# First batch's chunk loop: score matmuls two chunks ahead, weight conversions moved behind the loop, unread matmuls in every chunk

## The chip, the cores and the metric
The kernel runs on one core of one Trainium2 chip. The metric is the device time of one execution in microseconds. Five engines work side by side, each through its own list of instructions in order: PE (matmuls), DVE (vector), ACT (scalar functions), POOL (GpSimd) and SP, which here only starts transfers. An engine waits at an instruction until its inputs are there and its output buffer is free; what stands behind it on the same engine waits too.

## What is computed
The reference has three steps, for 4 batches of 768 positions with 8 heads of 48 channels (384 channels together). All is fp32.

```
# 1. scan over the positions t, for each head; a is complex, scaled to at most 0.999
S_re, S_im = ar*S_re - ai*S_im + outer(k_t, v_t),  ar*S_im + ai*S_re
y_t = q_t @ S_re
# 2. Fourier mixing over positions and channels, then a channel MLP
u = y + real(fft(fft(y, positions), channels))
z = u + relu(layernorm(u) @ w_ch1) @ w_ch2
# 3. a token MLP, then a channel MLP
z = z + (relu(z.T @ w_tok1) @ w_tok2).T
out = z + relu(z @ w_ch1') @ w_ch2'
```

## The kernel before, in words
**The scan.** The decay is the same for all positions of a short step, so the kernel first works out running products of `a` on DVE, ACT and POOL (for the next batch while the dense layers of this one run: the instructions around L558 to L615, of which L571 on POOL and L577 on DVE come early). Then the 768 positions are taken as 8 chunks of 96. A chunk `c` has four parts:
- `ch_load(c)`: SP starts the loads of V and of the scaled keys Kn. V has two buffers, so V(c+2) is loaded when the output of chunk c has been computed.
- `ch_sc(c)`: eight score matmuls q·k on PE (L753, two groups of four; a fp32 matmul shows as two entries in the trace, so one chunk is x16), and two masks on DVE (L760).
- `ch_u(c)`: V·K on PE (L768, L769) and then the state: DVE adds the old state (L779, `Aa`) and scales it (L785 `Xx`, L786 `yc`), POOL scales the other half (L787), DVE adds up the new state `T` (L789). Each chunk's state needs the one before: this is the chain of the loop.
- `ch_y(c)`: scores·V (L802) and q·T (L808) on PE, and ACT writes the chunk's output into `xT` (L810). After it stands `warm(n, ident)` where the table `WC` has a number n: n matmuls of 128x128 into a PSUM buffer that nobody reads (L309).

**Weight conversion.** The MLP weights come as fp64 bit patterns and are turned into two fp32r parts, high and low, in scratch memory. One conversion handles 128x384 weights: a 384 KB load by SP (L185), ACT L191 and L192, DVE L194, POOL L196, DVE L199, ACT L205, POOL L206, and a store by SP. Each needs the one before. Twenty of them (8 `early`, 12 `back`) are spread over the first batch; `tick` moves each running conversion on by one part and starts n new ones, `loads` starts only their loads, and `feed(n)` runs whatever of the twenty is left, in full. `CF[0]` are started ahead of the loop and `CF[c+1]` in chunk c. The other 36 are converted during the first dense layer.

**Stage 2, first batch.** `xT` is folded by sums and differences (`xf` L982, `xd` L988, `fd` L999; half on DVE, half on POOL for the first two), transformed by matmuls on PE (L1022, then L1033), copied out by ACT (L1069) and combined on POOL (L1070, L1071: three pairs). DVE joins that with the transposed x into u (L1085), takes mean and variance (L1092, L1093), refines the inverse root (L1104 to L1108) and normalizes (L1114), in three rounds. The normalized tiles are transposed on PE (L906), split by ACT (`th`, L909) and DVE (`tl`, L910), and the first MLP starts (L926, then ACT L930 and DVE L932; second layer L942).

**What sets the order.** The code is not run in the written order: a list scheduler with its own timeline orders each engine's instructions, and buffers come from pools by tag. `rests` and `after` are hints of order alone: in the loop, L194 and L199 come behind the chunk's T, and L196 behind its L787.

Of the kernel before, what the change touches and what calls it, by code (L numbers as in the profile page):

```python
# [26 lines left out]
SL4 = [(N4 * i, N4) for i in range(12)] + [(48, 1)]  # L27
ACL = 0.999
W0, WS = 2, 8
CF = (2, 2, 2, 2, 2, 0, 8, 0)  # L30
AN = (5, 6, 6, None)
WC = (0, 0, 0, 0, 0, 0, 10, 12)
WZ, CL = 0, 1
XL = (0,), (0, 1, 2, 3, 4, 5)
AH = 4
# [18 lines left out]
def attn_fft_mixer_kernel(ctx: ExitStack, tc: tile.TileContext, aL, xL, vL, wL, qN, kN, vN, arN, aiN,  # L54
# [37 lines left out]
    def alloc(tag, shape, dt=F32, name=None):  # L92
        n = 1
        for x in shape[1:]:
            n *= x
        t = pool.tile([128, SIZE[tag]], dt, tag=tag, bufs=BUFS[tag], name=name or tag)
        return shaped(t[0:shape[0], 0:n], shape)
# [3 lines left out]
    def palloc(tag, shape):  # L101
        n = 1
        for s in shape[1:]:
            n *= s
        t = psum.tile([128, 512], F32, tag=tag, bufs=PSB[tag], name=tag)
        v = t[0:shape[0], 0:n]
        if len(shape) == 3:
            v = v.rearrange("p (a b) -> p a b", b=shape[2])
        return v
# [107 lines left out]
    def begin():  # L217
        p, j = convs.pop(0)
        return convert(p, j, ws.place if (p, j) in early else None)
# [10 lines left out]
    def tick(n, loads=False):  # L230

        keep, stream[0] = stream[0], BACK
        active[:] = [g for g in active if next(g, "end") != "end"]
        for _ in range(n):
            g = begin()
            next(g)
            if not loads:
                next(g)
            active.append(g)
        stream[0] = keep  # L240
# [64 lines left out]
    def warm(n, x):  # L305

        ps = palloc("l", [128, 512])
        for _ in range(n):
            te.matmul(out=ps[:, 0:x.shape[1]], lhsT=ident[0:x.shape[0], :], rhs=x)  # L309
# [391 lines left out]
    def stage1(b):  # L701
# [9 lines left out]
        def st_g2():  # L711
            ps = palloc("s", [112, 4, 64])
            gt = alloc("e", [112, 3, 2, 64], name="gt")
            f47 = t[0]["ends"][:, 0].rearrange("p c f -> p (c f)")
            f48 = t[0]["ends"][:, 1].rearrange("p c f -> p (c f)")
            for j, (src, o, sel) in enumerate(((f47, 0, 64), (f47, 48, 64), (f48, 0, 0), (f48, 48, 0))):
                for r0 in (0, 64):
                    te.matmul(out=ps[r0:r0 + 48, j, :], lhsT=src[:, o:o + 48], rhs=ident[:, sel:sel + 64])

            def v(ap, r0):  # L720
                return ap[r0:r0 + 48].rearrange("p k (h c) -> p k h c", c=8)
            for r0 in (0, 64):
                fs, t1, t2, g = (v(x, r0) for x in (gt[:, 0], gt[:, 1], gt[:, 2], gm[b % 2]))
                se.copy(out=gt[r0:r0 + 48, 0], in_=ps[r0:r0 + 48, 0:2, :])
                bq = v(ps[:, 2:4, :], r0)
                ve.tensor_tensor(out=t1[:, :, :, 0:7], in0=fs[:, :, :, 0:7], in1=bq[:, :, :, 1:8], op=ALU.mult)
                for kk in range(2):
                    ve.tensor_tensor(out=t2[:, kk, :, 0:7], in0=fs[:, kk, :, 0:7], in1=bq[:, 1 - kk, :, 1:8], op=ALU.mult)
                ve.tensor_tensor(out=g[:, 0, :, 0:7], in0=t1[:, 0, :, 0:7], in1=t1[:, 1, :, 0:7], op=ALU.add)
                s0, s1 = (0, 1) if r0 == 0 else (1, 0)  # L730
                ve.tensor_tensor(out=g[:, 1, :, 0:7], in0=t2[:, s0, :, 0:7], in1=t2[:, s1, :, 0:7], op=ALU.subtract)
            fl = palloc("s", [128, 1])
            te.matmul(out=fl, lhsT=allones, rhs=good)
            ve.tensor_scalar(out=gate[:, b:b + 1], in0=fl, scalar1=127.5, scalar2=None, op0=ALU.is_ge)

        st = {}
        PU = "l" if b == 0 else "s"

        def ch_load(c):
            v = alloc("P", [96, 384], name="V")  # L740
            sp.dma_start(out=v, in_=vL[b, c])
            kt = alloc("A", [96, 8, 128], name="Kn")
            for hf in range(2):
                sp.dma_start(out=kt[48 * hf:48 * hf + 48],
                             in_=knd[hf].rearrange("(h c) s f -> c s h f", c=8)[c])
            st[c] = dict(v=v, kt=kt)

        def ch_sc(c, half):
            ps = palloc("s", [96, 4, 96])
            Q, K = qk[0][:, 1], qk[0][:, 0]  # L750
            for j in range(4):
                hc = (half * 4 + j) * 8 + c
                te.matmul(out=ps[:, j, :], lhsT=K[:, hc, :], rhs=Q[:, hc, :])  # L753
            sc = alloc("e", [96, 4, 96], name="sc")
            mb = mask.unsqueeze(1).to_broadcast([96, 4, 96])
            if half and OFF[2] & (1 << b):
                se.copy(out=sc, in_=ps)
                ge.tensor_tensor(out=sc, in0=sc, in1=mb, op=ALU.mult)
            else:
                ve.tensor_tensor(out=sc, in0=ps, in1=mb, op=ALU.mult)  # L760
            st[c][f"sc{half}"] = sc

        def ch_u(c):
            d = st[c]
            ps = palloc(PU, [112, 8, 48])
            for h in range(8):
                vv = d["v"][:, h * 48:h * 48 + 48]
                te.matmul(out=ps[0:64, h, :], lhsT=d["kt"][:, h, 0:64], rhs=vv)  # L768
                te.matmul(out=ps[64:112, h, :], lhsT=d["kt"][:, h, 64:112], rhs=vv)  # L769
            g = gm[b % 2].rearrange("p k (h c) -> p k h c", c=8)[:, :, :, c:c + 1]  # L770

            def gb(k, lo, hi):
                return g[lo:hi, k].to_broadcast([hi - lo, 8, 48])

            def v8(ap):
                return ap.rearrange("p (h e) -> p h e", e=48)
            if c:
                a = alloc("e", [112, 384], name="Aa")
                ve.tensor_tensor(out=v8(a), in0=v8(st["T"]), in1=ps, op=ALU.add)  # L779
                a = v8(a)  # L780
            else:
                a = ps
            y = yc[c % 2]
            x = alloc("e", [112, 384], name="Xx")
            ve.tensor_tensor(out=v8(x), in0=a, in1=gb(0, 0, 112), op=ALU.mult)  # L785
            (ge if c and b else ve).tensor_tensor(out=v8(y)[0:48], in0=a[64:112], in1=gb(1, 64, 112), op=ALU.mult)  # L786
            st["yop"] = (ge if c else ve).tensor_tensor(out=v8(y)[64:112], in0=a[0:48], in1=gb(1, 0, 48), op=ALU.mult)  # L787
            T = alloc("e", [112, 384], name="T")
            st["op"] = ve.tensor_tensor(out=T, in0=x, in1=y, op=ALU.add)  # L789
            st["Tn"] = T  # L790
            if b == 0:
                tops.append(st["op"])

        def ch_y(c):
            d = st[c]
            Q = qk[0][:, 1]
            ps = palloc(PU, [112, 4, 96])
            for p in range(4):
                for k in range(2):
                    h = 2 * p + k  # L800
                    m = 48 if k else 64
                    te.matmul(out=ps[64 * k:64 * k + m, p, :], lhsT=d["v"][:, h * 48:h * 48 + m],  # L802
                              rhs=d[f"sc{h // 4}"][:, h % 4, :], start=True, stop=(c == 0))
                if c:
                    for k in range(2):
                        h = 2 * p + k
                        m = 48 if k else 64
                        te.matmul(out=ps[64 * k:64 * k + m, p, :], lhsT=st["T"][:, h * 48:h * 48 + m],  # L808
                                  rhs=Q[:, h * 8 + c, :], start=False, stop=True)
            marked(se.activation(out=xT[:, :, c * 96:c * 96 + 96], in_=ps, func=ACTF.Copy, scale=gate[0:112, b:b + 1]))  # L810

        if b == 0:
            tick(CF[0])
        st_g2()
        ch_load(0)
        ch_load(1)
        ch_sc(0, 0)
        ch_sc(0, 1)
        for c in range(8):
            if c < 7:  # L820
                ch_u(c)
                ch_sc(c + 1, 0)
                ch_sc(c + 1, 1)
            ch_y(c)
            if b == 0 and WC[c]:
                warm(WC[c], ident)
            st["T"] = st.get("Tn")
            if c < 6:
                ch_load(c + 2)
            if b == 0 and c < 7:  # L830
                rests[0], rests[1] = tops[c], st["yop"]
                tick(CF[c + 1], c == 5)

# [120 lines left out]
    def stage2(b):  # L954
# [53 lines left out]
        if b == 0:  # L1008
            marked(x)
            rests[0], rests[1] = x, None  # L1010
            for _ in range(5):
                tick(0)
            rests[0] = None
# [38 lines left out]
        st = alloc("st", [128, 6, 6], name="bst")  # L1052
# [294 lines left out]
```

## Time and profile before
| | |
|---|---|
| median of 3 runs | 1103.9 us (1103.21 to 1104.33) |
| the profiled execution | 1103.4 us, of which the trace spans 1101.6 |
| busy in the span | PE 985.5 us (89%), DVE 784.3 (71%), ACT 506.2 (46%), POOL 387.3 (35%) |
| conversions in the whole run | L196 on POOL 56 times, 1163 ns each; L199 on DVE 56 times, 878 ns; L206 on POOL 44 times with the tile `w`, 1170 ns |
| mean granted PE clock | 0.955 of full speed |

The shares are means over stages with different limits. Times in the trace count from the start of the span; a row's last bracket says how long the engine idled before it and what ended the wait.

### The profile page before, as it was taken

Reading aid. Unit: us, or ns where it says so; the run is one execution under the profiler, and the core shown is the slowest. Engines: PE = TensorE matmul, PEld = TensorE weight load, DVE = VectorE, ACT = ScalarE, POOL = GpSimd, SP = SyncE. Lnnn points to the kernel's source line nnn. Section 1 sums busy time; section 2 is a strip of 40 time slices with the busy share of each in tenths; the row PEclk is TensorE's granted clock in tenths of the full one; section 3 lists DMA queues with packets and bytes.
Section 4 is the critical chain, followed back from the end, with each engine's and each line's share of the span. In section 5 each row is a group of like instructions: output and inputs, shape, how many; then the busy total and the mean of one; then the engine's idle time right before and its main releaser. Section 6 shows DMA issues by size and latency. Waiting matters only on the chain.

```text
span 1101.6 us, 21033 instructions
## 1 busy us (share of the span) xinstructions
PE 985.5 (89%) x7314; PEld 923.1 (84%) x7314; DVE 784.3 (71%) x2115; ACT 506.2 (46%) x1393; POOL 387.3 (35%) x520
## 2 busy tenths in 40 slices
PE   1368887999889999799998999999986999999997
PEld 0237775989788888699998899999976999999997
DVE  6986987999999668999767879985555433433332
ACT  6753355777876225867423567751124112121111
POOL 6643985573576444223226312211432002000000
PEclk9987797999999998899998999999988999999999
DMA  6137954686758664355565336655412433443432
GB/s 215 45 82 179 293 176 154 209 283 194 231 179 278 194 178 135 99 168 185 179 160 172 112 112 193 205 161 146 139 48 66 151 115 129 158 151 130 165 101 74
DMA packets 101536, 174.65 MB, mean 159 GB/s; under 512 B 11056, under 2 KB 61104, under 8 KB 100912
## 3 DMA queue, kind: packets, MB, share of 16 engines
q1 hardware_dynamic: 101424, 173.24, 51.1%
q8 instruction: 60, 0.98, 0.4%
q14 instruction: 52, 0.43, 0.1%
HBM read 133.88 MB, written 39.32 MB: 157 GB/s over the span
## 4 chain that ended last, share of the span: by engine, by line
PE 65%; DVE 10%; DMA 2%; ACT 1%; issue 1%; POOL 1%; SPq 0%; POOLq 0%; DVEq 0%; ACTq 0%
PE l L942 24%; PE l L926 22%; PE s L753 3%; PE s L642 2%; PE s L1033 2%; PE s L1022 2%; PE s L802 2%; DMA cvt<-wL 2%; PE s L808 1%; PE s L1147 1%; DVE ws L982 1%; PE s L1165 1%; PE s L768 1%; DVE cvt L199 1%; PE s L906 1%
## 5 line engine op out<-in xcount | busy, mean ns | idle before, releaser
L942 PE MATMUL l<-w,h 128*128 128x384 f32 x1728 | 332.5, 345 | 12.1 <-DVE h L932 8.4
L926 PE MATMUL l<-th,w 128*128 128x384 f32 x1152 | 314.4, 342 | 5.1 <-DVE h L932 2.6
L942 PEld LDWEIGHTS l<-w,h 128*128 128x128 f32 x1728 | 304.4, 192 | 16.8 <-DVE h L932 11.6
L926 PEld LDWEIGHTS l<-th,w 128*128 128x128 f32 x1152 | 210.8, 190 | 9.1 <-DVE h L932 4.1
L930 ACT ACTIVATE h<-l 128x384 fp32r<-128x384 f32 x192 | 94.0, 490 | 225.3 <-PE l L926 224.8
L926 PE MATMUL l<-tl,w 128*128 128x384 f32 x576 | 195.3, 339 | 0.0
L932 DVE SCALAR_TENSOR_TENSOR h<-l,h 128x384 fp32r<-128x384 f32 x192 | 106.2, 553 | 88.3 <-ACT h L930 87.9
L945 DVE TENSOR_TENSOR u<-u,l 128x384 f32<-128x384 f32 x192 | 105.4, 550 | 76.0 <-PE l L942 75.1
L926 PEld LDWEIGHTS l<-tl,w 128*128 128x128 f32 x576 | 109.1, 189 | 0.4 <-issue 0.2
L196 POOL TENSOR_TENSOR cvt<-cvt 128x384 int32<-128x384 int32 x56 | 64.8, 1163 | 38.2 <-DVE cvt L194 9.4
L466 PE MATMUL s<-misc,y 128*112 128x128 f32 x96 | 22.1, 377 | 52.1 <-DVE y L444 48.6
L753 PE MATMUL s<-qkt 112*96 112x96 f32 x512 | 59.7, 267 | 8.0 <-DVE sc L760 7.9
L466 PEld LDWEIGHTS s<-misc,y 128*112 128x112 f32 x96 | 14.5, 181 | 61.9 <-issue 27.3
L753 PEld LDWEIGHTS s<-qkt 112*96 112x96 f32 x512 | 53.4, 177 | 11.1 <-DVE sc L760 8.7
L786 POOL TENSOR_TENSOR yc<-Aa,gm 48x384 f32<-48x384 f32 x18 | 21.0, 1165 | 100.8 <-DVE Aa L779 100.8
L206 POOL TENSOR_TENSOR w<-cvt,w 128x384 fp32r<-128x384 f32 x44 | 51.1, 1170 | 10.5 <-ACT w L205 7.0
L199 DVE SCALAR_TENSOR_TENSOR cvt<-cvt 128x384 int32<-128x384 int32 x56 | 48.8, 878 | 7.0 <-POOL cvt L196 6.8
L1132 POOL TENSOR_TENSOR xl<-u,xh 128x384 fp32r<-128x384 f32 x18 | 17.9, 1004 | 101.1 <-ACT xh L1131 101.1
L571 POOL TENSOR_TENSOR tm<-tm 128x144 f32<-128x144 f32 (+1 forms) x51 | 26.6, 523 | 73.7 <-ACT tm L570 73.7
L642 PE MATMUL s<-misc,y 128*112 128x128 f32 x288 | 45.7, 275 | 1.5 <-DVE y L626 1.0
L615 DVE TENSOR_TENSOR p<-p,A 128x144 f32<-128x144 f32 x144 | 44.7, 310 | 2.0
L589 POOL TENSOR_TENSOR A<-raw,tm 128x144 f32<-128x144 f32 (+1 forms) x51 | 26.1, 513 | 56.0 <-DVE tm L587 29.4
(232 smaller groups left out, 1905.3 us busy)
## 6 DMA issues: line engine op xcount, KB each, us to landing
w<-wscr SPq DMA_DIRECT2D x180, 384.0 KB, 3.5
cvt<-wL SPq DMA_DIRECT2D x56, 384.0 KB, 4.7
wscr<-w SPq DMA_DIRECT2D x44, 384.0 KB, 3.2
Kn<-kn SPq DMA_DIRECT2D x64, 192.0 KB, 3.8
kn<-y SPq DMA_DIRECT2D x96, 96.0 KB, 2.7
raw<-aL SPq DMA_DIRECT2D x48, 144.0 KB, 3.0
xx<-xL SPq DMA_DIRECT2D x48, 144.0 KB, 3.2
V<-vL SPq DMA_DIRECT2D x32, 144.0 KB, 3.3
```

The lines of the kernel that those rows point to most:

```text
L196: x = ge.tensor_tensor(out=a, in0=a, in1=lo, op=ALU.add)
L199: rest(ve.scalar_tensor_tensor(out=a, in0=hi, scalar=-0x80000000, in1=a, op0=ALU.bitwise_and, op1=ALU.bitwise_or))
L206: ge.tensor_tensor(out=parts[:, 1, :], in0=a.bitcast(F32), in1=r32(parts[:, 0, :]), op=ALU.subtract)
L466: te.transpose(ps[:, j, :], y[:, j, 0:112], ident)
L615: ve.tensor_tensor(out=cur, in0=prev, in1=A[:, j, 0:3, :], op=ALU.mult)
L642: te.transpose(ps[:, j, :], y[:, j, 0:112], ident)
L753: te.matmul(out=ps[:, j, :], lhsT=K[:, hc, :], rhs=Q[:, hc, :])
L926: te.matmul(out=ps, lhsT=w1[:, wi, kt * 128:kt * 128 + 128], rhs=x[g][:, kt, :], start=(n == 0), stop=(n == 8))
L930: x = se.activation(out=hi, in_=ps, func=ACTF.Relu)
L932: ve.scalar_tensor_tensor(out=h[:, 1, g * 384:g * 384 + 384], in0=ps, scalar=0.0, in1=r32(hi), op0=ALU.max, op1=ALU.subtract)
L942: te.matmul(out=ps, lhsT=hs[m][:, hi, tt * 128:tt * 128 + 128], rhs=w2[:, wi, :], start=(n == 0), stop=(n == 8))
L945: ve.tensor_tensor(out=u[tt], in0=u[tt], in1=ps, op=ALU.add)
```

## The change
`CF` starts no conversions after chunks 2 and 3 of the first batch's loop, where it started two each, so four conversions leave the loop and six are left in it. The eight loads after chunk 5 stay. Behind the folds of stage 2 there are five more `tick(0)`, then `tick(6, True)`, which starts six conversions, and five more `tick(0)`; these six make up for the four that left the loop and for two that `feed` ran behind the normalization. The score matmuls of the first batch run two chunks ahead of the state. `WC` puts 4 unread matmuls behind the output matmuls of each of chunks 0 to 5; chunks 6 and 7 keep their 10 and 12. Nothing that is computed changes. Lines from L982 on stand 3 lines further down afterwards, those of stage 2 and the dense layers' callers behind the new ticks 6: `xf` is L985, `tl` L913, the POOL pair L1076 and L1077, the join L1091, the normalization L1120.

```diff
@@ -27,9 +27,9 @@
 SL4 = [(N4 * i, N4) for i in range(12)] + [(48, 1)]
 ACL = 0.999
 W0, WS = 2, 8
-CF = (2, 2, 2, 2, 2, 0, 8, 0)
+CF = (2, 2, 2, 0, 0, 0, 8, 0)
 AN = (5, 6, 6, None)
-WC = (0, 0, 0, 0, 0, 0, 10, 12)
+WC = (4, 4, 4, 4, 4, 4, 10, 12)
 WZ, CL = 0, 1
 XL = (0,), (0, 1, 2, 3, 4, 5)
 AH = 4
@@ -743,7 +743,7 @@
             for hf in range(2):
                 sp.dma_start(out=kt[48 * hf:48 * hf + 48],
                              in_=knd[hf].rearrange("(h c) s f -> c s h f", c=8)[c])
-            st[c] = dict(v=v, kt=kt)
+            st.setdefault(c, {}).update(v=v, kt=kt)
 
         def ch_sc(c, half):
             ps = palloc("s", [96, 4, 96])
@@ -758,7 +758,7 @@
                 ge.tensor_tensor(out=sc, in0=sc, in1=mb, op=ALU.mult)
             else:
                 ve.tensor_tensor(out=sc, in0=ps, in1=mb, op=ALU.mult)
-            st[c][f"sc{half}"] = sc
+            st.setdefault(c, {})[f"sc{half}"] = sc
 
         def ch_u(c):
             d = st[c]
@@ -814,13 +814,16 @@
         st_g2()
         ch_load(0)
         ch_load(1)
-        ch_sc(0, 0)
-        ch_sc(0, 1)
+        lead_sc = 2 if b == 0 else 1
+        for c in range(lead_sc):
+            ch_sc(c, 0)
+            ch_sc(c, 1)
         for c in range(8):
             if c < 7:
                 ch_u(c)
-                ch_sc(c + 1, 0)
-                ch_sc(c + 1, 1)
+            if c + lead_sc < 8:
+                ch_sc(c + lead_sc, 0)
+                ch_sc(c + lead_sc, 1)
             ch_y(c)
             if b == 0 and WC[c]:
                 warm(WC[c], ident)
@@ -1008,6 +1011,9 @@
         if b == 0:
             marked(x)
             rests[0], rests[1] = x, None
+            for k in range(5):
+                tick(0)
+            tick(6, True)
             for _ in range(5):
                 tick(0)
             rests[0] = None
```

The instructions on each engine move as follows; only order is shown here, no times. On PE, at the entry of the loop, the four score matmuls that stood between the ninth and tenth V·K matmul of chunk 0 are twelve afterwards. On ACT, the casts L191 and L192 of five of the eight weights loaded in chunk 5 stand ahead of the last chunk's output L810; before, four stood there.

**DVE, chunk 6** (names: `sc` score mask, `xf`, `xd` folds of stage 2, `cvt` conversion, `Aa`, `Xx`, `yc`, `T` the state). A piece of the difference:

```order
 L760 TENSOR_TENSOR sc<-s,misc 96x384 x2
-L982 TENSOR_TENSOR xf<-xT 112x4x96
-L199 SCALAR_TENSOR_TENSOR cvt<-cvt 128x384
-L988 TENSOR_TENSOR xd<-xf 112x2x96
+L985 TENSOR_TENSOR xf<-xT 112x4x96
+L991 TENSOR_TENSOR xd<-xf 112x2x96 x2
 L779 TENSOR_TENSOR Aa<-T,l 112x384
-L988 TENSOR_TENSOR xd<-xf 112x2x96
-L199 SCALAR_TENSOR_TENSOR cvt<-cvt 128x384
 L785 TENSOR_TENSOR Xx<-Aa,gm_81 112x384
 L786 TENSOR_TENSOR yc_79<-Aa,gm_81 48x384
 L789 TENSOR_TENSOR T<-Xx,yc_79 112x384
```

The conversions' L199 are gone from among the chunk's own operations; in chunk 5 one L194, one L199 ahead of `Xx`, another L199 and one more L194 are gone in the same way.

**POOL, stage 2** from the folds to the second pair (`ws` L1070/L1071, after L1076/L1077). Before:

```order
-L196 TENSOR_TENSOR cvt<-cvt 128x384 x6
-L206 TENSOR_TENSOR cvt<-cvt 128x384 x5
-L196 TENSOR_TENSOR cvt<-cvt 128x384
-L206 TENSOR_TENSOR cvt<-cvt 128x384
-L196 TENSOR_TENSOR cvt<-cvt 128x384
-L1070 TENSOR_TENSOR ws<-ws 128x193
-L1071 TENSOR_TENSOR ws<-ws 128x193
-L206 TENSOR_TENSOR cvt<-cvt 128x384
-L1070 TENSOR_TENSOR ws<-ws 128x193
-L1071 TENSOR_TENSOR ws<-ws 128x193
```

And afterwards:

```order
+L196 TENSOR_TENSOR cvt<-cvt 128x384 x8
+L206 TENSOR_TENSOR w<-cvt,w 128x384 x2
+L206 TENSOR_TENSOR cvt<-cvt 128x384 x6
+L1076 TENSOR_TENSOR ws<-ws 128x193
+L1077 TENSOR_TENSOR ws<-ws 128x193
+L196 TENSOR_TENSOR cvt<-cvt 128x384 x2
+L1076 TENSOR_TENSOR ws<-ws 128x193
+L1077 TENSOR_TENSOR ws<-ws 128x193
+L206 TENSOR_TENSOR cvt<-cvt 128x384 x2
+L196 TENSOR_TENSOR cvt<-cvt 128x384
```

Ahead of the first pair stood 14 conversion operations and now stand 16; between the first and the second pair one, now two.

**DVE, the end of the normalization** (`u` joined tile, `rs` the inverse root, `tl` the low part for the first MLP). Before, the last rows up to the next batch's scan (L577):

```order
-L1114 TENSOR_SCALAR ws<-u_1514,mv,rs 128x384
-L194 TENSOR_SCALAR cvt<-cvt 128x384
-L199 SCALAR_TENSOR_TENSOR cvt<-cvt 128x384
-L194 TENSOR_SCALAR cvt<-cvt 128x384
-L910 TENSOR_TENSOR tl<-s,th 128x3x128 x2
-L199 SCALAR_TENSOR_TENSOR cvt<-cvt 128x384
```

And afterwards, the third round, ahead of its L1120:

```order
+L913 TENSOR_TENSOR tl<-s,th 128x3x128
+L1091 TENSOR_TENSOR u_1505<-s,ws 1x192
+L194 TENSOR_SCALAR cvt<-cvt 128x384
+L199 SCALAR_TENSOR_TENSOR cvt<-cvt 128x384
+L1098 BN_STATS bst<-u_1502 128x6
+L194 TENSOR_SCALAR cvt<-cvt 128x384
+L1098 BN_STATS bst<-u_1505 128x6
+L913 TENSOR_TENSOR tl<-s,th 128x3x128
+L1099 BN_AGGR mv<-bst 128x2
+L199 SCALAR_TENSOR_TENSOR cvt<-cvt 128x384
```

From the first join to the last normalization no conversion stood on DVE; afterwards there are six L199 and four L194, and none between the last normalization and L577, where two of each stood.

## Rows read from the trace of the kernel before

**Rows 1.** The page, part 4: the chain that ended last, by engine
```profile
PE 65%; DVE 10%; DMA 2%; ACT 1%; issue 1%; POOL 1%; SPq 0%; POOLq 0%; DVEq 0%; ACTq 0%
```

**Rows 2.** Windows: length; busy PE, PEld, DVE, ACT, POOL; granted clock; DMA share, GB/s
```profile
85.66:97.11 11.45, 9.97 (x114) 9.18 (x115) 6.50 (x21) 0.84 (x2) 0.00 (x0) 0.57 0.41 83
97.11:144.54 47.43, 37.45 (x518) 34.88 (x519) 41.50 (x63) 19.74 (x42) 41.79 (x33) 0.82 0.96 289
144.54:170.42 25.88, 23.68 (x151) 19.13 (x149) 21.20 (x28) 12.77 (x35) 22.70 (x22) 0.93 0.45 169
170.42:183.91 13.49, 7.49 (x40) 5.41 (x40) 12.94 (x50) 6.62 (x18) 4.37 (x7) 0.76 0.34 117
191.41:350.00 158.59, 147.80 (x852) 138.91 (x851) 153.86 (x436) 120.47 (x340) 97.65 (x127) 1.00 0.70 225
350.00:1101.60 751.60, 719.45 (x5495) 689.95 (x5493) 477.06 (x1270) 283.73 (x778) 166.85 (x236) 0.97 0.47 143
```

**Rows 3.** Timeline of DVE, chunks of batch 0: start, length, instruction, idle before
```profile
97.11 0.55 DVE L779 TENSOR_TENSOR Aa<-T,l 112x384 f32<-112x384 f32 x1 [0.94 <-PE l L769]
...
122.44 0.56 DVE L789 TENSOR_TENSOR T<-Xx,yc 112x384 f32<-112x384 f32 x1 [1.81 <-POOL yc L787]
...
122.92 1.01 DVE L760 TENSOR_TENSOR sc<-s,misc 96x384 f32<-96x384 f32 x2
...
130.32 1.34 DVE L789 TENSOR_TENSOR T<-Xx,yc 112x384 f32<-112x384 f32 x1
...
138.94 1.18 DVE L789 TENSOR_TENSOR T<-Xx,yc 112x384 f32<-112x384 f32 x1
...
144.57 0.86 DVE L982 TENSOR_TENSOR xf<-xT 112x384 f32<-112x384 f32 x1 [1.51 <-ACT xT L810]
```

**Rows 4.** Timeline of PE, chunks of batch 0 and the first dense matmul
```profile
100.91 1.60 PE L753 MATMUL s<-qkt 112*96 112x96 f32 x16
...
120.66 0.29 PE L769 MATMUL l<-V,Kn 96*48 96x48 f32 x1
...
122.49 2.88 PE L753 MATMUL s<-qkt 112*96 112x96 f32 x16
...
133.03 0.58 PE L802 MATMUL l<-sc,V 96*64 96x96 f32 x4
...
135.78 2.80 PE L309 MATMUL l<-misc 128*128 128x128 f32 x20
...
141.49 1.61 PE L309 MATMUL l<-misc 128*128 128x128 f32 x12
...
186.23 1.38 PE L926 MATMUL l<-th,w 128*128 128x384 f32 x3 [0.65 <-ACT th L909]
```

**Rows 5.** Timeline of ACT, end of the chunks
```profile
140.37 0.56 ACT L192 ACTIVATE cvt<-cvt 128x384 int32<-128x384 uint32 x1
...
143.96 0.58 ACT L810 ACTIVATE xT<-l,gate 112x384 f32<-112x384 f32 x1 [3.04 <-PE l L808]
```

**Rows 6.** DMA view of 127 to 139 us: queue SP, count, size, microseconds to landing
```profile
cvt<-wL SPq DMA_DIRECT2D x6, 384.0 KB, 5.1
```

**Rows 7.** Timeline of POOL in stage 2
```profile
160.69 5.70 POOL L206 TENSOR_TENSOR cvt<-cvt 128x384 fp32r<-128x384 f32 x5
...
169.56 0.52 POOL L1070 TENSOR_TENSOR ws<-ws 128x193 f32<-128x193 f32 x1
```

**Rows 8.** Timeline of DVE in stage 2 and up to the next scan
```profile
152.03 1.69 DVE L194 TENSOR_SCALAR cvt<-cvt 128x384 int32<-128x384 int32 x6
...
154.63 7.79 DVE L199 SCALAR_TENSOR_TENSOR cvt<-cvt 128x384 int32<-128x384 int32 x6 [0.90 <-POOL cvt L196]
...
185.37 0.83 DVE L199 SCALAR_TENSOR_TENSOR cvt<-cvt 128x384 int32<-128x384 int32 x1 [1.19 <-POOL cvt L196]
...
187.95 1.35 DVE L199 SCALAR_TENSOR_TENSOR cvt<-cvt 128x384 int32<-128x384 int32 x1 [0.25 <-POOL cvt L196]
...
191.41 0.80 DVE L577 SCALAR_TENSOR_TENSOR tm<-tm 128x144 f32<-128x144 f32 x2 [2.11 <-POOL tm L571]
```

## Prediction
> **What bounds the kernel now.** The chain that ended last names PE for 65% of the span and DVE for 10% [rows 1], but an average over stages says little about a change in one of them, so I read the windows next [rows 2]. They show who is full where. From 350 us on PE is busy 719.45 of 751.60 us: nothing the change does is there, and it can only start earlier or later. From 191.41 to 350, where the next batch's scan runs beside the first dense layer, DVE is busy 153.86 of 158.59 and PE 147.80: DVE bounds it, PE is close behind. So what counts is when that stretch can start: on DVE with L577 at 191.41 [rows 8], on PE with the first dense matmul at 186.23 [rows 4]. Ahead of it lie three stages. In the chunks (97.11 to 144.54) DVE is busy 41.50 of 47.43 and POOL 41.79: both are nearly full, with a granted PE clock of 0.82. From `xT` complete to the first join (144.54 to 170.42) POOL has 22.70 of 25.88, much of it conversions (five L206 in a row alone are 5.70 [rows 7]). In the normalization (170.42 to 183.91) DVE has 12.94 of 13.49 and POOL only 4.37. The rows of DVE give the pace of the chunks [rows 3]: the state T ends at 123.00, 131.66 and 140.12 for chunks 4, 5 and 6, that is 8.7 and 8.5 us a chunk, and the last `xT` lets the folds start at 144.57.
>
> **The change, part by part.** I follow one time through the stages: how much later (+) or earlier (-) each ends.
>
> *Entry of the loop.* Eight more score matmuls stand ahead of the rest of the first V·K. At the half clock level, which the stretch 85.66 to 97.11 mostly has (0.57) [rows 2], sixteen entries take 2.88 us, at full 1.60 [rows 4]: +2.9. The eight that follow (of chunk 2 instead of chunk 1) should then run at full level: -1.3. The four unread matmuls in front of the next V·K are eight entries of 1.61/12 = 0.134: +1.1. The first `Aa` of the chain, which waits for PE now (0.94 idle at 97.11) [rows 3], comes 2.7 later. Bounds: 1.1 if the scores fit into waits of PE, 4.0 if the clock does not gain. The gain of scores two ahead, that DVE's masks never wait for PE, is worth little, since DVE's idle time in the whole loop is 47.43 - 41.50 = 5.9 us, and the row that shows most of one such wait names POOL (1.81 at 122.44). I keep chunks 1 to 4 at their pace: six conversions are still spread over them.
>
> *Chunks 5 and 6.* The four conversions that leave had their DVE and POOL parts there. T4 to T6 took 17.1 us. What stays on DVE is, for chunk 5, two masks (1.01 [rows 3]), `Aa`, `Xx`, `yc` and T, each 0.55 alone (the row of `Aa`), up to 1.34 beside POOL (the T of 130.32), and for chunk 6 also one `xf` and two `xd`. Alone that makes 3.2 + 4.5 = 7.7; all at prices beside POOL 10.6. POOL has much less to do there, so I take 8.7, nearer the lower end: -8.4. T6 then ends at 140.1 + 2.7 - 8.4 = 134.4.
>
> *The last `xT`.* It came 4.4 after T6 (144.54 = 143.96 + 0.58 [rows 5]), with unread matmuls between its pieces; in one piece some 2.5 are enough: 136.9. But on ACT the casts of five fresh loads stand ahead of it. Before, the casts ended at 140.9 and ACT then idled 3.04 for PE [rows 5], so they cost nothing; now they may. The loads leave SP behind V(7), which waits for the output of chunk 5, at about 128. Loads here land after 5.1 us [rows 6], and four more of 393 KB each at the loop's 289 GB/s [rows 2] would come 1.36 apart. All five within 5.1 gives 133, one behind the other 138.5; I take 136, then two casts of 0.56, then the output: 137.7, say 137.5. That is -7.0 against 144.54. Bounds: 0.6 earlier, 2.7 later. This is where part of the gain of the loop already stops.
>
> *POOL ahead of the first pair.* From the last `xT` to L1070 it took 25.0 us (144.54 to 169.56 [rows 7]), POOL full. Sixteen conversion operations instead of fourteen: two more L206 at 5.70/5 = 1.14 [rows 7], +2.3. Left: -4.7. DVE, ACT and PE have room there (21.20, 12.77 and 23.68 of 25.88 [rows 2]).
>
> *The normalization.* Here six L199 and four L194 now stand in DVE's list, which has 0.55 us of idle time in 13.49 [rows 2]. An L194 is 1.69/6 = 0.28. An L199 is 0.55 where nothing is beside it (as `Aa`, an operation of like size), 7.79/6 = 1.30 in a row beside POOL's L206, and 0.83 and 1.35 in the two that stood behind the last normalization [rows 8], where POOL works on and off, as it will here; their mean 1.09 is my price. 6 x 1.09 + 4 x 0.28 = 7.7, less 0.55 idle: +7.1. Bounds of the work: 4.4 and 8.9. Left: +2.4 at the last normalization.
>
> *Behind it.* The two conversions that `feed` ran there are gone. L577 waited 2.11 for POOL's L571 [rows 8], which stood behind their last L206, and that behind the L199 of 187.95. Without these 1.35 + 1.14 = 2.5 the scan starts at 2.4 - 2.5 = -0.1. The first dense matmul gets back only what two casts of ACT took ahead of the `th` for which it waited (0.65 [rows 4]), some 0.8 of 1.1: +1.6.
>
> *Sum.* DVE, which bounds the next stretch, starts 0.1 earlier, PE 1.6 later, and PE has 10.8 us of room in it. I take +0.5, a third of the way. The profiled execution took 1103.4, so 1103.9; it lies 0.5 under the median of the runs shown, so **1104.4** as a median. In short: the work that left the loop is the same work, on the same two engines, and it lands in the one later stretch where DVE has no room.
>
> **A rule on the clock.** The stretch ahead of the loop has PE busy 9.97 of 11.45 at 0.57, the loop 37.45 of 47.43 at 0.82, the stretch from 191.41 on 147.80 of 158.59 at 1.00 [rows 2]: the clock rises behind dense PE work and falls back in the loop. The Trainium skill, page "TensorE: Matmul & The Clock Gate", section "What's actually happening", says that the throttled state is the default and that activity releases it; by it the unread matmuls should lift the loop's clock, and the entry's -1.3 is safe, while the second rival below is unlikely. No row here shows a loop with them.
>
> **The rivals.**
> *A, faster: the loop's gain survives.* The conversions in the normalization cost their lower bound (4.4 in place of 7.7, since POOL is busy there only 4.37 of 13.49 now) and the loads do not hold up the last `xT` (-0.6): 1104.4 - 3.3 - 0.6 = 1100.5. For it speaks POOL's light load, against it that the conversions bring POOL's work along. With chunks 1 to 4 quicker too, as far as 1098.5.
> *B, slower: PE becomes the bound of the chunks.* At half level V·K takes 1.83 (120.66 to 122.49), scores 2.88, outputs 2.75 (133.03 to 135.78) [rows 4], and four unread matmuls twice 1.07: 9.6 us a chunk, over today's 8.5 and far over the 3.6 to 5.1 I want for chunks 5 and 6. It decides if the clock is at half through either of them: +9.6 - 4.4 = +5.2, 1109.6. Against it: the clock needs to stay low in a PE that is then always busy.
> *C, slower: L199 in the normalization waits for POOL.* DVE takes its list in order, so each L199 that stands ahead of a join or a `tl` and whose L196 is late stops the normalization; idle times of 1.19 and 0.25 for just this are there behind the normalization now [rows 8]. Four of the six L199 belong to L196 that POOL runs between its pairs. At 1.0 each: +4.0, 1108.4. It decides from two such waits on.
> *D, slower: the loads.* The fifth load lands at 138.5: +2.7, 1107.1.
> *E, nothing:* the moves cancel, as in my sum.
>
> **Chances and range.** A change of under 0.2% (2.2 us) can't be told from none here. My forecast (E, 1101.7 to 1106.1) gets 0.36; A 0.35; B 0.07; C 0.14; D 0.08. So faster 0.35, same 0.36, slower 0.29. The range reaches to most of A and C: 1098.5 to 1109.0; the forecast's own is 1101.7 to 1106.1.
>
> **What would show it.** Right: `Aa` of chunk 1 some 2.7 later on DVE; T5 and T6 together about 8.7 behind T4; the last L810 on ACT near 137.5, its wait named after a load or PE; first L1076 some 27 after it; DVE 20 us from first join to last L1120; L577 near 191.3. Wrong, for A: that last stretch under 18 us. For B: granted clock under 0.7 between T4 and T6, and PE busy throughout. For C: idle rows of DVE inside the normalization with POOL's `cvt` L196 as releaser. For D: the last L810 behind L192 with no idle time in front. If chunks 1 to 4 change their pace by more than a microsecond each, the first term is wrong, and with it everything behind.

## The result and the profile after

The changed kernel takes 1115.0 us (median of 4 runs, 1113.7 to 1118.1) against 1103.6 before: a ratio of 1.0109 with an interval of 1.0086 to 1.0133. It is slower by about 11 us, outside the range of the prediction. The profiled execution took 1113.7, of which the trace spans 1112.0, 10.4 more than before.

The windows of after, cut at the same events as [rows 2] (columns as there):

```profile
85.66:99.84 14.18, 12.51 (x138) 11.56 (x138) 7.49 (x23) 0.84 (x2) 0.00 (x0) 0.65 0.42 84
99.84:137.85 38.01, 35.00 (x541) 32.23 (x542) 35.07 (x51) 15.45 (x33) 29.45 (x27) 0.96 0.85 258
137.85:166.04 28.19, 22.40 (x151) 17.73 (x149) 20.92 (x33) 13.98 (x39) 23.55 (x22) 1.00 0.51 178
...
166.04:187.75 21.71, 9.34 (x40) 6.53 (x40) 21.17 (x59) 11.80 (x29) 15.81 (x17) 0.61 0.60 230
192.38:353.79 161.41, 147.37 (x837) 137.76 (x835) 154.33 (x427) 118.33 (x335) 96.40 (x126) 0.99 0.67 216
353.79:1112.00 758.21, 720.51 (x5514) 691.17 (x5514) 480.58 (x1278) 283.59 (x783) 167.67 (x238) 0.98 0.48 143
```

The chunks are 9.4 us shorter (38.01 against 47.43) at a granted clock of 0.96 in place of 0.82; the stretch ahead of them is 2.7 longer, POOL's stretch 2.3 longer, the normalization 8.2 longer (21.71 against 13.49), with DVE full in it (21.17) and POOL busy 15.81 in place of 4.37. That is the first batch: it comes out 3.8 us late at the last normalization and 1.0 late at the next scan. The rows of DVE give the same, event by event:

```profile
99.84 0.56 DVE L779 TENSOR_TENSOR Aa<-T,l 112x384 f32<-112x384 f32 x1 [1.05 <-PE l L769]
...
123.73 0.56 DVE L789 TENSOR_TENSOR T<-Xx,yc 112x384 f32<-112x384 f32 x1
...
127.50 1.17 DVE L789 TENSOR_TENSOR T<-Xx,yc 112x384 f32<-112x384 f32 x1
...
133.34 1.17 DVE L789 TENSOR_TENSOR T<-Xx,yc 112x384 f32<-112x384 f32 x1
...
182.97 0.51 DVE L199 SCALAR_TENSOR_TENSOR cvt<-cvt 128x384 int32<-128x384 int32 x1
...
184.41 1.31 DVE L199 SCALAR_TENSOR_TENSOR cvt<-cvt 128x384 int32<-128x384 int32 x1
...
187.28 0.47 DVE L1120 TENSOR_SCALAR ws<-u,mv,rs 128x384 f32<-128x384 f32 x1
...
192.38 0.80 DVE L577 SCALAR_TENSOR_TENSOR tm<-tm 128x144 f32<-128x144 f32 x2 [1.83 <-POOL tm L571]
```

T of chunk 6 ends at 134.5 (before 140.1 [rows 3]), the last normalization at 187.75 (before 183.91), and the next batch's scan starts at 192.38, one microsecond later than the 191.41 of [rows 8]. The rows of ACT, POOL and PE that answer to [rows 5], [rows 7] and [rows 4]:

```profile
136.84 0.55 ACT L192 ACTIVATE cvt<-cvt 128x384 int32<-128x384 uint32 x1
137.28 0.57 ACT L810 ACTIVATE xT<-l,gate 112x384 f32<-112x384 f32 x1
...
165.37 0.52 POOL L1076 TENSOR_TENSOR ws<-ws 128x193 f32<-128x193 f32 x1
...
189.33 0.69 PE L929 MATMUL l<-th,w 128*128 128x384 f32 x1
```

The last `xT` comes directly behind a cast on ACT (no idle time in front), at 137.85; the first pair on POOL stands at 165.37; the first dense matmul at 189.33, 3.1 later than before. So at this point the kernel is 1 to 3 us late. At the end it is 10.4 late. The other 7 to 9 us come in stretches in which the change altered no instruction: from the scan's start to the last y of the scan (L626 of the trace's sixteenth step, at 345.9 before and 353.8 after) it took 154.5 us before and 161.4 after, with the same work. Another 2.5 come in single stages behind that.

What did change there is order. The scheduler lays out the whole program with its own timeline, and behind stage 2 of the first batch, where both kernels are written alike instruction for instruction, 2543 of PE's 5296 places, 1325 of DVE's 1706, 765 of ACT's 1125, 94 of POOL's 368 and 295 of SP's 549 differ between the two.

### The profile page after: what moved, and what is told of

It reads as the page before. It is cut to its first block, busy times and chain, and to the rows that moved or that the text cites. A ratio compares the mean times of both kernels' runs of the same rounds, so it can differ in the third digit from the quotient of the medians.

```text
span 1112.0 us, 21117 instructions
## 1 busy us (share of the span) xinstructions
PE 986.0 (89%) x7362; PEld 921.3 (83%) x7362; DVE 787.8 (71%) x2115; ACT 503.9 (45%) x1393; POOL 382.6 (34%) x520
## 4 chain that ended last, share of the span: by engine, by line
PE 66%; DVE 19%; ACT 4%; DMA 4%; POOL 3%; issue 2%; SPq 0%; POOLq 0%; DVEq 0%; ACTq 0%
PE l L929 22%; PE l L945 22%; PE s L753 4%; PE s L642 2%; DMA cvt<-wL 2%; PE s L1039 2%; PE s L1028 2%; PE s L802 2%; DVE cvt L199 2%; POOL cvt L196 1%; DVE ws L991 1%; PE s L808 1%; PE s L1153 1%; DVE ws L985 1%; PE s L768 1%
## 5 line engine op out<-in xcount | busy, mean ns | idle before, releaser
L945 PE MATMUL l<-w,h 128*128 128x384 f32 x1728 | 323.7, 339 | 14.2 <-DVE u L948 10.7
L929 PE MATMUL l<-th,w 128*128 128x384 f32 x1152 | 317.6, 343 | 7.1 <-DVE h L935 4.9
L945 PEld LDWEIGHTS l<-w,h 128*128 128x128 f32 x1728 | 298.6, 189 | 19.9 <-DVE u L948 13.4
L929 PEld LDWEIGHTS l<-th,w 128*128 128x128 f32 x1152 | 209.9, 189 | 11.9 <-DVE h L935 7.3
L929 PE MATMUL l<-tl,w 128*128 128x384 f32 x576 | 194.5, 338 | 0.0
L935 DVE SCALAR_TENSOR_TENSOR h<-l,h 128x384 fp32r<-128x384 f32 x192 | 106.1, 553 | 93.3 <-ACT h L933 92.8
L948 DVE TENSOR_TENSOR u<-u,l 128x384 f32<-128x384 f32 x192 | 104.9, 548 | 69.6 <-PE l L945 69.3
L929 PEld LDWEIGHTS l<-tl,w 128*128 128x128 f32 x576 | 108.7, 189 | 0.3 <-DVE tl L913 0.3
L196 POOL TENSOR_TENSOR cvt<-cvt 128x384 int32<-128x384 int32 x56 | 65.5, 1177 | 41.6 <-DVE cvt L194 9.2
L753 PE MATMUL s<-qkt 112*96 112x96 f32 x512 | 57.1, 261 | 1.5 <-DVE sc L760 1.5
L199 DVE SCALAR_TENSOR_TENSOR cvt<-cvt 128x384 int32<-128x384 int32 x56 | 51.5, 930 | 4.5 <-POOL cvt L196 4.1
L206 POOL TENSOR_TENSOR w<-cvt,w 128x384 fp32r<-128x384 f32 x44 | 48.7, 1115 | 4.1 <-ACT w L205 3.8
L642 PE MATMUL s<-misc,y 128*112 128x128 f32 x288 | 45.9, 277 | 0.0
```

The costliest lines, as they stand in the source:

```text
L196: x = ge.tensor_tensor(out=a, in0=a, in1=lo, op=ALU.add)
L199: rest(ve.scalar_tensor_tensor(out=a, in0=hi, scalar=-0x80000000, in1=a, op0=ALU.bitwise_and, op1=ALU.bitwise_or))
L206: ge.tensor_tensor(out=parts[:, 1, :], in0=a.bitcast(F32), in1=r32(parts[:, 0, :]), op=ALU.subtract)
L642: te.transpose(ps[:, j, :], y[:, j, 0:112], ident)
L929: te.matmul(out=ps, lhsT=w1[:, wi, kt * 128:kt * 128 + 128], rhs=x[g][:, kt, :], start=(n == 0), stop=(n == 8))
L935: ve.scalar_tensor_tensor(out=h[:, 1, g * 384:g * 384 + 384], in0=ps, scalar=0.0, in1=r32(hi), op0=ALU.max, op1=ALU.subtract)
```

## The experiments

In the tables and rows of held kernels the line numbers are some 229 higher, since the table of the order stands at the head of the file: L1158 is the first dense matmul L929 there, L1164 its ReLU L935, L1174 L945, L1177 L948, L1400 L1171, L871 L642.

**The order behind stage 2, held.** All instructions written behind stage 2 of the first batch are chained, engine by engine, in an order read from the other kernel's program. A link orders two instructions on one engine and adds no wait. The first batch's own order stays as it was, place for place.

```diff
+    byname = {i.name: i for i in nc.cur_bb.bb.instructions}
...
+        for p, q in zip(seq, seq[1:]):
+            tc.add_manual_dep(byname[f"I-{q}"], f"I-{p}", HOLD, reason="pinned order")
```

Changed kernel in the order of before:

> The changed kernel, with every instruction written behind stage 2 of the first batch held in the order of the kernel before on each engine (order hints alone, 9000 instructions). Theory R (the loss behind 192 us comes from the other order that the scheduler gave to the same instructions): only the delay at the start of the next scan and of the first dense matmul is left, +1 to +3, so 1104.5 to 1107 us. Theory W (the loss follows from the later start and from what collides then, in any order): 1113 to 1116 us, as the changed kernel.

Measured: 1103.9 us, ratio 1.0011 (0.9997 to 1.0024). And the kernel before in the order of the changed one:

> The mirror: the kernel before, its first batch unchanged, with every instruction behind stage 2 of the first batch held in the order of the changed kernel. Theory R: scan start stays near 191.4, the loss behind it comes all the same: 1109 to 1113 us. Theory W: no change, 1102 to 1105 us.

Measured: 1115.3 us, ratio 1.0101 (1.0084 to 1.0118). The two results lie 0.6 us below and 2.3 us above the ranges of theory R, both on the side away from W. Theory W falls and R stands: the order that the scheduler gave to the untouched instructions makes the loss, in either kernel; without it the change is worth nothing. The window from the scan's start to the last y of the scan shows where. Kernel before:

```profile
191.41:345.86 154.45, 144.10 (x831) 135.71 (x830) 149.75 (x426) 117.98 (x333) 93.95 (x124) 1.00 0.69 225
```

The changed kernel with the order of before:

```profile
191.16:346.50 155.34, 147.01 (x839) 139.01 (x839) 150.15 (x426) 118.19 (x334) 94.17 (x125) 0.99 0.68 221
```

The kernel before with the order of the changed one:

```profile
192.85:354.49 161.64, 147.46 (x835) 138.24 (x833) 153.31 (x427) 117.97 (x335) 96.63 (x126) 0.98 0.67 218
```

155.3 and 161.6: the stretch takes the length that goes with its order, whichever first batch ran ahead of it. DVE's work in it is some 4 us longer for the same instructions (153.31 against 149.75, 154.33 against 150.15). PE, with the same instructions, idles 14.0 of 161.4 us in the changed kernel and 8.3 of 155.3 when its order is held; in the kernel before it idles 10.4 of 154.5, and 14.2 of 161.6 with the order of the changed one. What PE waits for there, by the view of waits (engine, line, releaser: microseconds in total, times, longest). Changed kernel:

```profile
PE l L929 <- DVE h L935: 4.9, 7, 1.4
PE l L945 <- DVE h L935: 2.1, 2, 1.6
PE l L945 <- DVE u L948: 2.1, 2, 1.3
PE l L1171 <- ACT R L1159: 1.8, 1, 1.8
PE l L929 <- DVE u L948: 1.4, 2, 1.1
```

Changed kernel with the order of before:

```profile
PE l L1158 <- DVE h L1164: 2.2, 2, 1.9
PE l L1400 <- ACT R L1388: 1.5, 1, 1.5
PE s L871 <- DVE y L855: 1.0, 2, 0.7
PE l L1158 <- DVE u L1177: 0.9, 1, 0.9
PE l L1174 <- DVE h L1164: 0.9, 1, 0.9
```

Kernel before:

```profile
PE l L926 <- DVE h L932: 2.4, 3, 1.9
PE l L942 <- DVE h L932: 2.1, 2, 1.1
PE l L1165 <- ACT R L1153: 2.0, 1, 2.0
PE l L926 <- DVE u L945: 1.4, 2, 0.9
```

The kernel before with the order of the changed one (L1154 is the first dense matmul, L1170 the second layer's):

```profile
PE l L1154 <- DVE h L1160: 4.5, 7, 1.4
PE l L1170 <- DVE u L1173: 2.3, 3, 1.4
PE l L1170 <- DVE h L1160: 2.1, 2, 1.6
PE l L1393 <- ACT R L1381: 2.1, 1, 2.1
PE l L1154 <- DVE u L1173: 1.3, 2, 1.0
```

In these two layers the rows that wait for `h` or `u` of DVE make 4.9 + 2.1 + 2.1 + 1.4 = 10.5 us in the changed kernel and 2.2 + 0.9 + 0.9 = 4.0 with its order held; with the other first batch they make 2.4 + 2.1 + 1.4 = 5.9 and, in the changed order, 4.5 + 2.3 + 2.1 + 1.3 = 10.2. So the order adds 6.5 us of such waits where the stretch is 6.1 longer, and 4.3 where it is 7.2 longer. How such a wait comes about is seen on DVE of the changed kernel:

```profile
241.39 1.35 DVE L199 SCALAR_TENSOR_TENSOR cvt<-cvt 128x384 int32<-128x384 int32 x1
242.67 0.25 DVE L617 TENSOR_TENSOR p<-p,yt 128x96 f32<-128x96 f32 x1
242.96 0.32 DVE L615 TENSOR_TENSOR p<-p,A 128x144 f32<-128x144 f32 x1
243.31 0.26 DVE L616 TENSOR_TENSOR yt<-p,A 128x96 f32<-128x96 f32 x1
243.48 0.55 DVE L935 SCALAR_TENSOR_TENSOR h<-l,h 128x384 fp32r<-128x384 f32 x1
```

and on its PE:

```profile
244.09 0.44 PE L929 MATMUL l<-th,w 128*128 128x384 f32 x1 [1.39 <-DVE h L935]
```

A conversion's L199 and three operations of the scan stand in DVE's list ahead of the ReLU that frees PE's buffer; the L199 takes 1.35, where the shortest of this kernel took 0.51; DVE is never idle, and PE is, for 1.39.

**The parts of the change, order free.** In the first, the conversions alone are moved:

```diff
-WC = (4, 4, 4, 4, 4, 4, 10, 12)
+WC = (0, 0, 0, 0, 0, 0, 10, 12)
...
-        lead_sc = 2 if b == 0 else 1
+        lead_sc = 1
```

> The changed kernel without the unread matmuls of chunks 0 to 5 and with scores one chunk ahead: only the conversions are moved. Entry of the loop as before, so the first Aa of the chain at 97.1 instead of 99.8 and the chunks 5 and 6 short; if the entry's 2.7 us are carried through, the next scan starts at 189.5 to 190. Theory W: the total follows that start, 1101 to 1104 us. Theory R: the scheduler orders all that follows anew, and the total may lie anywhere between 1098 and 1115 us, whatever the start.

In the second only the unread matmuls are taken away from the changed kernel (the first two lines of the diff):

> The changed kernel without the unread matmuls of chunks 0 to 5, scores still two ahead. By my price the first Aa comes 1.1 earlier than in the changed kernel (98.7); if the clock falls for want of them, chunks 2 to 4 are slower by up to 1 us each and T of chunk 4 ends at 124 to 127. The next scan starts at 191 to 193. Theory W: total 1112 to 1116; theory R: free of the start, 1098 to 1115 us.

In the third the scores two ahead stand alone, in the fourth the unread matmuls:

```diff
-CF = (2, 2, 2, 0, 0, 0, 8, 0)
+CF = (2, 2, 2, 2, 2, 0, 8, 0)
...
-            for k in range(5):
-                tick(0)
-            tick(6, True)
```

> Only the scores two chunks ahead, conversions and unread matmuls as before. It orders what follows in its own way, closer to the kernel before than the changed kernel is (773 instead of 2543 of PE's places differ). The entry costs 1.2 to 2.2 at the first Aa of the chain, the next scan starts at 191 to 193. If only the order behind it decides, the total is not told by that start: 1102 to 1115 us; if it were the start, 1103 to 1105.

> Only the four unread matmuls in each of chunks 0 to 5. First Aa 1.1 later by my price, granted clock in the chunks above 0.82, chunks at the pace before or up to 0.5 us quicker each; next scan at 190.5 to 192.5. The order behind it is close to that of the changed kernel, so 1111 to 1116 us if the order decides, 1102 to 1105 if the start does.

**The same parts, the order behind held in that of before:**

> Scores two chunks ahead alone, with all five lists behind stage 2 in the order of the kernel before. In the unheld kernel of the same first batch the next scan started at 188.9, 2.5 earlier than before, and the first dense matmul 1.1 earlier. If only order and start count (theory R), the total follows the start: 1100.5 to 1102.5 us, a little faster than before. If the order of the kernel before fits only its own start (theory F), 1104 or more.

> The moved conversions alone, order behind held. Unheld: next scan +0.9, first dense matmul +3.0. Theory R: 1103.5 to 1106 us. Theory F: 1107 or more. This also prices my terms for the chunks, POOL and the normalization: none of them gains.

> The unread matmuls alone, order behind held. Unheld: next scan +7.0, first dense matmul +8.7, total +1.5%. Theory R: the start's part stays, 1109 to 1112 us, and the other 8 to 9 us go. Theory F: 1114 or more.

> Scores two ahead and unread matmuls, conversions as before, order behind held. Its first batch has not run yet. Theory R: the total stands as far from 1103.5 as the next scan and the first dense matmul stand from 191.4 and 186.2 (between the two), within 1 us.

All results, each with the start of the next scan (L577's first row) and of the first dense matmul in its own trace. "Behind" is the span less the scan's start, that is everything that the change does not touch; these three columns are of one execution each.

| kernel | scan | matmul | behind | median us | ratio (interval) |
|---|---|---|---|---|---|
| before | 191.4 | 186.2 | 910.2 | 1103.6 | |
| changed | 192.4 | 189.3 | 919.6 | 1115.0 | 1.0109 (1.0086 to 1.0133) |
| conversions alone | 192.3 | 189.3 | 920.0 | 1112.7 | 1.0074 (1.0050 to 1.0098) |
| without unread | 191.3 | 188.3 | 922.2 | 1115.1 | 1.0097 (1.0080 to 1.0114) |
| scores ahead alone | 188.9 | 185.1 | 916.7 | 1112.4 | 1.0087 (1.0055 to 1.0118) |
| unread alone | 198.4 | 195.0 | 922.5 | 1120.7 | 1.0150 (1.0121 to 1.0179) |
| before, order of changed | 192.8 | 187.7 | 921.9 | 1115.3 | 1.0101 (1.0084 to 1.0118) |
| changed, order of before | 191.2 | 188.2 | 910.6 | 1103.9 | 1.0011 (0.9997 to 1.0024) |
| conversions alone, held | 189.9 | 186.8 | 910.4 | 1105.2 | 1.0016 (1.0002 to 1.0030) |
| scores ahead alone, held | 190.8 | 187.0 | 913.1 | 1104.9 | 1.0023 (1.0003 to 1.0043) |
| unread alone, held | 197.2 | 193.8 | 911.5 | 1110.6 | 1.0060 (1.0047 to 1.0073) |
| scores and unread, held | 194.5 | 190.6 | 911.1 | 1107.4 | 1.0034 (1.0021 to 1.0046) |

In its profiled execution every kernel with the order of before takes 910 to 913 us behind the scan's start, every one with an order of its own or that of the changed kernel 917 to 922, whether its scan starts at 188.9 or at 198.4. Theory F falls for the conversions and for the unread matmuls, and scores and unread matmuls together come out at +3.9, between their +3.1 and +4.4, as theory R has it: the order of before serves other starts as well, up to 6 us later. The scores ahead alone are the miss: their free run had the earliest start of all and still lost 0.9%, but held they were expected a little faster than before and came out 0.2% slower, where theory F had put them. Three things meet there, and the runs don't part them: the scan starts at 190.8 in the held execution and at 188.9 in the free one, with the same first batch, so that most of the gain read from the free trace was that execution's; the rest behind it took 913.1, 2.9 longer than before; and single runs lie far apart, from 1107.1 to 1118.9 free and from 1101.8 to 1111.4 held, so that for this first batch a single run is good to some 10 us only, in either order. The kernel without unread matmuls has, behind stage 2, the order of the changed kernel in every place, and the same time (1115.1 and 1115.0).

With the order free, the conversions alone and the scores alone lie in the wide ranges that go with the order, and outside those that go with the start. Without the unread matmuls 1115.1 is at the upper end of theory R's range and inside theory W's, so that run does not part the two. The unread matmuls alone lie above both their ranges (1120.7 against 1111 to 1116). Three of the four starts of the scan are misses: 192.3 for the conversions (189.5 to 190 expected), 188.9 for the scores (191 to 193) and 198.4 for the unread matmuls (190.5 to 192.5).

The unread matmuls alone, which I had priced at 1.1, make the scan start 5.8 to 7.0 later; together with the scores 3.1, and with everything else of the change nothing that can be told (191.3 without them, 190.3 to 192.4 with them). In the two traces with the unread matmuls alone the T of chunk 6 ends 1.1 and 1.3 late, the last `xT` 3.0 and 3.5, the last normalization 8.8 and 7.6. The parts do not add up; each has a first batch ordered anew, too, and no run holds that order.

**Which list carries it.** The changed kernel with one, two or three of the five lists held in the order of before, and the kernel before with only DVE's list in that of the changed one (the edit is that of the first diff, with the lists of the other engines left empty):

> The changed kernel with only DVE's 1706 instructions behind stage 2 of the first batch held in the order of the kernel before; PE, ACT, POOL and SP are ordered anew around it. If DVE's list carries the loss (theory D: PE waits for ReLU and sum operations that stand behind conversions and scan operations on DVE), 1103 to 1106 us, near the kernel with all five lists held; if the loss needs the lists of the other engines too (theory O), 1109 us or more.

> The mirror: the kernel before with only DVE's list behind stage 2 in the order of the changed kernel. Theory D: 1112 to 1116 us. Theory O: 1103 to 1108 us.

> The changed kernel with only PE's 5296 instructions behind stage 2 in the order of the kernel before; 654 of DVE's places, 431 of ACT's and 85 of POOL's then still differ. If PE's list carries the loss, 1103 to 1106 us; if DVE's does as much, 1108 us or more.

> The changed kernel with DVE's and PE's lists held and ACT, POOL and SP free (113, 16 and 24 places differ). If these two carry the loss together, 1103 to 1106 us, as with all five held; if ACT, POOL or SP hold what the held DVE list alone left (6.6 us), 1108 to 1111 us.

> As the kernel before this one, ACT's list held too: only POOL and SP are free. If ACT's order makes the difference between the two, this one is at 1103 to 1105.5 us and the other is not; if the conversions on POOL or the loads on SP make it, both stay at 1108 or more.

| kernel | lists held | behind | median us | ratio (interval) |
|---|---|---|---|---|
| changed | DVE | 917.9 | 1110.2 | 1.0066 (1.0045 to 1.0087) |
| changed | PE | 913.1 | 1108.0 | 1.0024 (1.0006 to 1.0042) |
| changed | DVE, PE | 916.0 | 1109.3 | 1.0036 (1.0020 to 1.0053) |
| changed | DVE, PE, ACT | 911.5 | 1105.6 | 1.0012 (0.9992 to 1.0031) |
| before | DVE, of the changed | 921.2 | 1114.6 | 1.0102 (1.0074 to 1.0129) |

The expectations took it that one list carries the loss, and these runs don't show one that does. DVE's list of the changed kernel brings all of it to the kernel before, where theory D had put it. But the other lists are ordered around it, and all but 16 of PE's places, 119 of ACT's and 19 of POOL's came out as in the changed kernel, so this run does not part DVE's list from the rest. DVE's list of before takes only 40% of the loss away, though it leaves only 111 of PE's, 222 of ACT's, 17 of POOL's and 37 of SP's places different. PE's list alone takes three quarters (1108.0, between the two outcomes that were expected), and DVE's added to it takes no more. With ACT's added to both, nothing is left that can be measured; but the intervals with and without ACT's list overlap, so its share is not shown either. That the lists cost by how they fit each other is the reading that is left, argued and not shown. Single runs of the partly held kernels also lie further apart (1106.8 to 1116.3 with DVE's held).

A version that beats both kernels did not come up: none of the sixteen is faster than before.

## Why the prediction was wrong

The step that failed is the last of the sum: "DVE, which bounds the next stretch, starts 0.1 earlier, PE 1.6 later, and PE has 10.8 us of room in it. I take +0.5", and behind it the sentence on the stretch from 350 us on, "nothing the change does is there, and it can only start earlier or later". It takes the length of everything behind the scan's start as given. It is given only for a given order, and here the new order, without any time, already had half of PE's places and three quarters of DVE's changed. That length went from 910.2 to 919.6. With the order held it is 910.6 and the whole change measures 1.0011 (0.9997 to 1.0024), within which the +0.5 of the sum lies.

Point by point, the measured number in the changed kernel's profiled execution behind the predicted one:
- *Entry:* `Aa` of chunk 1 at +2.7, measured +2.7 (99.84). The exact hit is luck: in the six executions of this first batch, free, held and partly held, `Aa` lay between 97.8 and 99.8, that is +0.7 to +2.7.
- *Chunks 5 and 6:* T of chunk 6 at 134.4, measured 134.5. Two errors cancel in it: chunks 1 to 4 did not keep their pace but won 1.4 (T of chunk 4 at +1.3 instead of +2.7), and chunks 5 and 6 took 10.2 instead of 8.7. The upper price of 10.6 in that term does not follow from its rows: twice the masks at 1.01 and four operations at 1.34 make 12.7 already.
- *The last `xT`:* 137.5, measured 137.85, and it did stand behind a fresh load's casts on ACT, as the gate in the sum has it. The sign set for rival D, no idle time behind L192, came with it, but D's price did not: the sign could not tell D from the sum.
- *POOL:* first pair at 164.8, measured 165.4.
- *Normalization:* +7.1, measured +8.2 (21.71 less 13.49), with six L199 between 0.51 and 1.31 us; the last normalization at +3.8 instead of +2.4, +2.7 with the order held. Idle time was 0.54, as before, and no row there waits for an L196, so rival C's waits of DVE did not come. The six L199 sum to 4.8 and the four L194 to 2.0, that is 6.7 against the 7.7 priced; the other operations of the stretch took some 1.5 longer, which the sum has not, and none of the work went into the idle time.
- *Scan and first dense matmul:* -0.1 and +1.6; measured +1.0 and +3.1, and -0.2 and +2.0 with the order held. The spread is wider than the difference from before: the scan starts at 190.3 to 192.4 in the six executions of this first batch, and at 190.6 to 192.8 in the three of the batch of before.
- *Rival B:* it did not come; between T4 and T6 the granted clock was 1.00. From the first `Aa` to the last `xT` it rose from 0.82 to 0.96. That the unread matmuls did it is not shown: the conversions alone, with none in chunks 0 to 5, have 0.96 free and 0.91 held, the unread matmuls alone 0.90 and 0.86. Nor is a gain seen from it: the conversions alone took 41.93 us there at 0.96 and 39.65 at 0.91. The Trainium skill, page "TensorE: Matmul & The Clock Gate", section "What's actually happening", has activity release the throttle; no run here tests which activity did.

So the sum of the first batch holds to 1 or 2 us, in part by terms that cancel and within the spread of its executions, and the work that left the loop came back in the normalization as the prediction said. The loss has another cause, which was no rival in it.

Open: which rows of the order cost what. Waits of PE for ReLU and sum operations on DVE grow by 4.3 to 6.5 us, and DVE's own work by some 4, in the stretch where 6 to 7 of the 9 us are lost; both are seen, but no run changed single rows. Nor is it known whether the order of before is a rare good one: five other first batches gave four orders (the changed kernel and the one without unread matmuls share theirs), all 0.7 to 1.5% slower. Not every edit brings a new order: one unread matmul fewer behind chunk 7 of the kernel before leaves every place behind stage 2 as it was, while in the changed kernel it moves 813 of PE's (neither was run, so only the order is known).

## What to carry to other kernels

Where a scheduler with a timeline orders the program, an edit in one stage is two edits: its own, and a new order for everything behind it. Compare the order of the untouched part before a sum is made against its length, and give the new order a case of its own. To measure the edit itself, hold the order of the rest; to keep a good order, hold it as well, since here it was worth more than any part of the edit.

## What the runs showed of the hardware that I had not expected

The same DVE instructions cost 149.75 us in one order and 153.31 in another (the scan with the first dense layer, kernel before in both). The 56 L199 of the changed kernel ran between 0.51 and 1.42 us each; in the kernel before their median was 0.64, and 0.81 with the order of the changed one. DVE's idle time does not show that, since it stands in the durations. And the same first batch, place for place, let the scan start some 2 us apart in two executions: 192.3 and 189.9 for the moved conversions, 188.9 and 190.8 for the scores ahead. In the ten runs of the scores ahead alone, one program, the five of 1110.1 us or less have a mean granted clock of 0.957 to 0.965 and the five of 1114.7 or more 0.946 to 0.952; which of the two brings the other is not shown.
